# Clamps of a weight preparation on GpSimd and a new, strictly followed order for the attention of an attention, soft MoE and MLP kernel

## The chip, the cores and the metric

The kernel runs on one core of a Trainium2 chip. The time is that of one execution on the device, in microseconds. A core has a matmul engine (TensorE, PE in the rows; its weight loads are PEld), three others that work in parallel with it (VectorE or DVE, ScalarE or ACT, GpSimd or POOL), and SyncE (SP), whose queue issues nearly all DMA transfers here. Each engine takes its instructions strictly in the order in which the program gives them, and waits on semaphores for the others.

## What is computed

```python
# 4 batches, 8 heads, 576 tokens, head size 64; float32 throughout
q_rot, k_rot = rotate(q), rotate(k)              # rotary embedding
scores = q_rot @ k_rot.T / 8
attn = exp(scores - scores.max(-1)); attn /= attn.sum(-1) + 1e-9
x = (attn @ v) -> (2304, 512)                    # heads side by side
logits = x @ phi                                 # 32 slots, 8 experts x 4
d = softmax(logits, over tokens); slot_in = d.T @ x
slot_out[e] = relu(slot_in[e] @ w1[e]) @ w2[e]   # 512 -> 1024 -> 512
x = softmax(logits, over slots) @ slot_out
out = relu(x @ w_in) ** 2 @ w_out                # 512 -> 2048 -> 512
```

w_in and w_out come as 64-bit floats, and the kernel turns them into float32.

## The kernel before

The attention works on 16 pairs of heads. The two heads of a pair lie in the upper and lower 64 partitions, so that two matmuls with 64 rows of contraction run side by side. For each pair:

- rope_pair (L547) rotates k and q with six operations of 128x576 on GpSimd (for pair 0 on VectorE). parts_pair (L571) splits each into a rounded part "hi" (ScalarE) and a rest "lo" (GpSimd), so that f32r products of parts make up a more exact product; windows (L629) keeps copies of the last 64 keys.
- max_unit (L642): a hi x hi product for each of four blocks of 128 keys and two halves of the queries, and one for the last 64 keys of both halves: nine products, each a pair of f32r matmuls (the last has two pairs) into one of three PSUM bank pairs, the "ring"; VectorE reduces each to a maximum (L665). max_rows (L670) transposes the maxima (L684), and SyncE writes them as a row "mrow" into the operand tile (L703).
- st_unit (L727): the score products of the same nine units. Each takes three pairs of f32r matmuls for the parts (L738) and one that subtracts the maximum (L745), twice as many for the last unit; ScalarE takes the exponential of the ring bank (L758) into one of a few probability buffers, whose key in the planner is pk. GpSimd adds the buffers of units 0 and 1 (L766).
- pv_unit (L774): the product with V in float32, two matmuls of 64 columns side by side (L789); the unit of the last 64 keys has its own form (L784). norm (L795): column sums (L813) and their inverse on VectorE. logits (L849): products with phi (L863, L868) and transposes of the result (L886). After each fourth pair slots_in (L902) updates the slots.

free (L1153) loads expert weights in pieces of 512 KB into buffers as these come free: ten of a ring, w0 to w9, others in tiles that the attention gives up at its end (arena, tO, tEa, tEb, tLa, tLb, pb). prepare (L1194) converts an eighth of the weights that stay in DRAM as float32: load, scale to z (ScalarE, L1213), low half (ScalarE, L1220), clamp of z (VectorE, L1225), upper half (ScalarE, L1232), shift and merge (VectorE, L1237), store (SyncE, L1244). Behind the attention experts (L1412) multiplies with w1 and w2, whose later pieces are loaded as buffers come free, and mlp (L1610) does the rest.

What sets the order: every operation goes into a Plan (L30) with its engine, a cost in us, a due time, and what it reads and writes. emit (L292) simulates the engines with these costs: of the operations that are ready and can start within 0.208 us (AHEAD, TensorE) of the earliest, it issues the one that is due first. For the attention the due times come from ORDER, a table of ranks by function and engine (retime, L221); they are preferences. "soft" operations give way when a hard one is due in the meantime. In gaps of TensorE that the plan foresees, emit puts filler products (L1880). What is issued is a fixed program; the chip knows nothing of ranks and costs.

Of the kernel before, what the change touches and what calls it, by code (L numbers as in the profile page):

```python
# [38 lines left out]
class Plan:  # L39
# [14 lines left out]
            0, 2, 3, 4  # L54
        ),
        ("first_loads", "ACT", None): (
            1,
        ),
        ("first_loads", "DVE", None): (
            20,  # L60
        ),
        ("rope_pair", "DVE", None): (
            11, 12, 15, 13, 16, 18
        ),
        ("warm_up", "PE", None): (
            14,
        ),
        ("parts_pair", "ACT", None): (
            17, 19, 55, 79, 117, 150, 194, 224, 273, 305, 346, 361, 429, 454, 526, 531, 631, 633, 721, 724, 815, 818, 910, 914, 1013, 1015, 1101, 1104, 1193,
            1196, 1261, 1268  # L70
        ),
        ("parts_pair", "POOL", None): (
            22, 28, 60, 86, 124, 160, 199, 230, 279, 314, 359, 369, 435, 460, 532, 543, 637, 648, 732, 742, 825, 836, 922, 929, 1023, 1032, 1112, 1120, 1202,
            1210, 1273, 1281
        ),
        ("rope_pair", "POOL", None): (
# [4 lines left out]
        ),  # L81
        ("load", "SP", None): (
            36, 99, 173, 176, 180, 237, 240, 242, 322, 323, 327, 373, 377, 379, 468, 471, 473, 557, 561, 565, 659, 662, 665, 753, 755, 758, 846, 849, 852, 942,
            946, 949, 1043, 1045, 1047, 1131, 1133, 1136
        ),
        ("windows", "ACT", None): (
            23, 30, 82, 81, 156, 132, 226, 217, 309, 296, 406, 408, 499, 502, 606, 608, 698, 701, 791, 794, 884, 887, 988, 990, 1078, 1081, 1168, 1171, 1265,
            1275, 1331, 1332
        ),
# [7 lines left out]
        ),  # L97
        ("max_unit", "DVE", None): (
# [6 lines left out]
        ),  # L105
        ("max_rows", "DVE", None): (
            43, 47, 48, 56, 58, 59, 122, 129, 133, 205, 215, 218, 297, 306, 308, 395, 409, 412, 487, 500, 503, 593, 609, 610, 688, 702, 703, 779, 795, 796, 874,
            888, 889, 975, 991, 993, 1068, 1082, 1083, 1156, 1172, 1173, 1249, 1264, 1266, 1348, 1352, 1353, 1403, 1409, 1414
        ),
        ("max_rows", "PE", "f"): (  # L110
            46, 57, 127, 211, 302, 405, 498, 605, 697, 790, 883, 987, 1077, 1167, 1260, 1349, 1406
        ),
        ("max_rows", "SP", None): (
            51, 62, 134, 136, 219, 222, 312, 317, 415, 417, 509, 510, 615, 618, 707, 710, 800, 803, 893, 896, 997, 1000, 1087, 1090, 1177, 1180, 1270, 1274, 1358,
            1355, 1422, 1418
        ),
        ("max_rows", "ACT", None): (
            52, 63
        ),
        ("<lambda>", "SP", None): (  # L120
            65,
# [91 lines left out]
            0: 1514, 1: 1524, 2: 1526  # L213
        },
        (None, "ACT", None): {
            0: 1525
        },
    }
    kind = None
# [26 lines left out]
    def op(self, engines, fn, due, reads=(), writes=(), kb=None, after=None, spare=None, take=None, give=None, wait=0.0, behind=None, tok=None, mode=None, like=None, soft=False):  # L246
# [7 lines left out]
        i = len(self.ops)  # L254
# [1717 lines left out]
```

## Time and profile before

| | us |
|---|---|
| median of 3 runs | 565.54 |
| lowest, highest | 565.38, 566.69 |
| the profiled execution | 565.09 |
| its span, first to last instruction | 563.3 |
| TensorE busy in it | 544.0 |
| VectorE, ScalarE, GpSimd busy | 398.6, 295.7, 229.9 |

The span covers first to last instruction; the 1.8 us of the execution beside it are its start and end. A view "windows" gives the busy time of each engine in a stretch, "timeline" the instructions in order of time. In a timeline row the first number is the start, the second the time taken, "xN" the count of like instructions merged into the row, and the brackets hold the idle time of the engine ahead of it and what ended it. A float32 matmul of the program appears as two in the trace, one of f32r as one. Ends of matmuls are modelled; starts are measured.

### The profile page before, as it was taken

The numbers are of one execution on the slowest core, as the hardware profiler recorded it, in microseconds if no ns is written. First come the engines' busy times: TensorE is split into PE (matmuls) and PEld (weight loads), VectorE is DVE, ScalarE is ACT, GpSimd is POOL, SyncE is SP. The second block draws the span as 40 slices with busy tenths as digits, with TensorE's granted clock in tenths as the row PEclk, the third lists the DMA queues.
The fourth block names the chain that finished last, engine by engine and source line by source line (L and its number), as shares of the span: only waits on it lengthen the run. The fifth ranks groups of instructions, "written<-read, shape, count | busy, mean of one in ns | idle before, by whom it ended". The sixth has DMA issues, their size and how long they took to land.

```text
span 563.3 us, 13271 instructions
## 1 busy us (share of the span) xinstructions
PE 544.0 (97%) x5406; PEld 416.7 (74%) x5406; DVE 398.6 (71%) x878; ACT 295.7 (52%) x568; POOL 229.9 (41%) x178
## 2 busy tenths in 40 slices
PE   4999999999999999999999999999999999999996
PEld 3656666566665666666642258999999999999996
DVE  6587788888897887876468748965775595554553
ACT  2334545664555655544426548975944564354440
POOL 4999999988889788723610000000000000000000
PEclk9999999999999999999999999999999999999999
DMA  7447796877784357222989997132200220000333
GB/s 237 139 132 184 167 249 188 221 192 195 210 219 117 93 144 201 100 99 101 338 295 396 409 401 255 39 111 76 76 1 1 76 76 2 1 1 1 113 113 112
DMA packets 37741, 85.68 MB, mean 152 GB/s; under 512 B 12176, under 2 KB 12848, under 8 KB 36528
## 3 DMA queue, kind: packets, MB, share of 16 engines
q1 hardware_dynamic: 37398, 84.24, 48.3%
q8 instruction: 42, 0.69, 0.5%
q10 hardware_dynamic: 282, 0.59, 0.4%
q14 instruction: 19, 0.16, 0.1%
HBM read 77.92 MB, written 6.82 MB: 150 GB/s over the span
## 4 chain that ended last, share of the span: by engine, by line
PE 81%; DMA 9%; DVE 5%; POOL 2%; ACT 1%; issue 1%; SPq 0%; DVEq 0%
PE bank L1806 35%; PE bank L738 11%; PE obank L789 11%; PE bank L654 5%; PE bank L813 5%; PE bank L745 3%; PE obank L1736 3%; DVE mcol L665 2%; DMA w__1345<-in_w_dram 2%; DMA tEb<-in_w_dram 2%; DMA tLb<-in_w_in_dram 2%; PE obank L784 2%; PE bank L886 2%; DMA ident<-in_ident_dram 1%; POOL arena L543 1%; DMA w__448<-in_w_dram 1%
## 5 line engine op out<-in xcount | busy, mean ns | idle before, releaser
L758 ACT ACTIVATE tO<-bank 128x576 f32<-128x576 f32 x140 | 84.2, 650 | 84.4 <-PE bank L745 83.3
L665 DVE TENSOR_REDUCE mcol<-bank 128x2 f32<-128x576 f32 x144 | 103.2, 749 | 22.6 <-PE bank L654 13.1
L543 POOL TENSOR_TENSOR arena<-arena 128x576 f32<-128x576 f32 x78 | 111.0, 1444 | 8.8 <-DMA arena<-in_qk_dram 8.0
L1806 PE MATMUL bank<-w,tEb 128*128 128x256 f32 x864 | 106.5, 279 | 0.1
L1806 PEld LDWEIGHTS bank<-w,tEb 128*128 128x128 f32 x864 | 103.5, 188 | 2.4 <-issue 1.6
L789 PE MATMUL obank<-tO,pb 128*64 128x288 f32 x496 | 74.8, 419 | 0.0
L766 POOL TENSOR_TENSOR pb<-tO 128x576 f32<-128x576 f32 x30 | 42.9, 1430 | 31.0 <-ACT tO L758 29.4
L1806 PE MATMUL bank<-w,tEa 128*128 128x256 f32 x432 | 53.0, 278 | 0.0
L1806 PEld LDWEIGHTS bank<-w,tEa 128*128 128x128 f32 x432 | 51.6, 188 | 1.2 <-issue 1.2
L1806 PE MATMUL bank<-w,tO 128*128 128x256 f32 x432 | 51.6, 277 | 0.0
L1806 PEld LDWEIGHTS bank<-w,tO 128*128 128x128 f32 x432 | 51.1, 188 | 0.0
L789 PEld LDWEIGHTS obank<-tO,pb 128*64 128x64 f32 x496 | 29.8, 136 | 22.7 <-issue 9.3
L1747 ACT ACTIVATE pb<-obank 128x384 f32<-128x384 f32 x47 | 21.7, 495 | 36.8 <-PE obank L1736 36.8
L1747 ACT ACTIVATE w__1091<-obank 128x384 f32<-128x384 f32 x48 | 21.8, 491 | 36.5 <-PE obank L1736 36.2
L654 PEld LDWEIGHTS bank<-tEb 64*128 64x128 f32 x180 | 16.3, 184 | 21.5 <-DVE mcol L665 4.4
L813 PE MATMUL bank<-tO,ones 128*32 128x288 f32 x224 | 31.9, 409 | 0.0
L654 PE MATMUL bank<-tEb 64*128 64x288 f32 x180 | 30.5, 355 | 0.7 <-DVE mcol L665 0.5
L819 DVE STREAM_TRANSPOSE bank<-bank 128x288 f32<-128x288 f32 x32 | 15.9, 496 | 19.2 <-PE bank L813 15.8
L543 POOL TENSOR_TENSOR tLb<-arena,tEb 128x576 fp32r<-128x576 f32 x20 | 28.6, 1448 | 1.3 <-ACT tEb L577 1.3
L738 PE MATMUL bank<-tEb 64*128 64x288 f32 x180 | 28.5, 313 | 0.3 <-DVE mcol L665 0.2
L1736 PE MATMUL obank<-x,tO 128*128 128x384 f32 x95 | 26.8, 336 | 0.5 <-DVE tO L1664 0.5
L738 PE MATMUL bank<-tLb,tEb 64*128 64x288 f32 x180 | 26.6, 292 | 0.0
(299 smaller groups left out, 1095.2 us busy)
## 6 DMA issues: line engine op xcount, KB each, us to landing
arena<-in_qk_dram SPq DMA_DIRECT2D x14, 576.0 KB
arena<-in_qk_dram SPq DMA_DIRECT2D x12, 512.0 KB
arena<-in_w_dram SPq DMA_DIRECT2D x8, 512.0 KB
pb<-in_v_dram SPq DMA_DIRECT2D x12, 320.0 KB
arena<-in_qk_dram SPq DMA_DIRECT2D x3, 1152.0 KB
tLb<-in_w_in_dram SPq DMA_DIRECT2D x3, 1024.0 KB
pb<-in_w_in_dram SPq DMA_DIRECT2D x3, 1024.0 KB
w__448<-in_w_dram SPq DMA_DIRECT2D x4, 512.0 KB
```

What stands on the lines that cost most here:

```text
L543: ENG[e].tensor_tensor(out=o, in0=x, in1=y, op=how)
L654: nc.tensor.matmul(on_ring(tok)[:, j, 0:HQ], lhsT=x[rows], rhs=hi[rows, 0, HALF[c]], start=(u < BOTH or c == 0), stop=(u < BOTH or c == 1),)
L665: lambda e: nc.vector.tensor_reduce(out=mcol[:, h, :, u], in_=on_ring(tok)[:, :, 0:HQ], op=ALU.max, axis=AX.X),
L738: nc.tensor.matmul(st[:, j, 0:HQ], lhsT=w[rows], rhs=q[y][rows, HALF[c]], start=(i == 0 and (u < BOTH or c == 0)), stop=False,)
L745: nc.tensor.matmul(st[:, j, 0:HQ], lhsT=pick[rows, w : w + 128], rhs=mrow[rows, HALF[c]], start=False, stop=(u < BOTH or c == 1),)
L758: lambda e: nc.scalar.activation(out=pr, in_=on_ring(tok)[:, :, 0:HQ], func=AF.Exp, scale=0.125),
L766: lambda e: nc.gpsimd.tensor_tensor(out=acc, in0=one, in1=pr, op=ALU.add),
L789: nc.tensor.matmul(BANKS[6 + h][o, 0:HQ], lhsT=vr[:, u, j, :], rhs=pr[:, j, :], start=(h == 0 and u == 0), stop=(h == 1 and u == 3))
L813: nc.tensor.matmul(sm[QUAD[2 * j + w], 0:HQ], lhsT=one, rhs=x[:, j, :], start=(i == 0), stop=(i + w + 2 > last))
L1736: lambda e, i=i, t0=t0: nc.tensor.matmul(BANKS[i][:, 0:384], lhsT=wst_of()[:, 128 * fc : 128 * fc + 128], rhs=cst_of()[:, t0 : t0 + 384], ...
L1747: lambda e, i=i, h=h: nc.scalar.activation(out=rg_of()[:, 0, h], in_=BANKS[i][:, 0:384], func=AF.Relu),
L1806: nc.tensor.matmul(BANKS[c][:, cols], lhsT=gt[:, x, 128 * c : 128 * c + 128], rhs=wo[:, fc % 2, y, cols], start=(fc % FQ == 0 and i == 0 a ...
```

## The change

Five edits. ORDER has new ranks, and they are now followed strictly: retime collects (rank, operation), and emit takes the next of this list, asserts that it is ready, and issues it, with no choice; the greedy rule is left for what has no rank, that is all behind the attention. The clamp of prepare goes from VectorE to GpSimd, and is no longer soft. Each st_unit names its probability buffer pk among its writes, where it did so for the last two pairs alone. Three VectorE costs of the plan are raised. The plan holds GpSimd while VectorE runs an operation with "lock". Behind the planner's part the diff shows in turn rope_pair (the shift of prepare gets the same lock), max_rows, st_unit, two places of norm, and prepare.

```diff
     ORDER = {
         ("first_loads", "SP", None): (
-            0, 2, 3, 4
+            1, 4, 20, 8
         ),
...
+        ("prepare", "POOL", None): (
+            605, 610, 692, 778, 940, 1010, 1051, 1193
+        ),
...
     def retime(self):
         count = {}
+        self.turn = []
...
             if kind or n in ranks:
-                self.ops[i] = (*o[:2], 0.1 * ranks[n], *o[3:])
+                self.turn.append((ranks[n], i))
...
+        turn = [i for _, i in sorted(self.turn, reverse=True)]
         while ready:
             cand = []
-            for i in ready:
+            ranked = turn.pop() if turn else None
+            assert ranked is None or ranked in ready, (ranked, self.kinds[ranked])
+            for i in ready if ranked is None else (ranked,):
...
-            if i in self.soft:
+            if i in self.soft and ranked is None:
...
+            alone = i in self.locks and e == "DVE"
+            if alone:
+                start = max(start, free.get("POOL", 0.0))
             end = start + self.ops[i][0][e]
+            if alone:
+                free["POOL"] = end
...
-                    spare={"DVE": T["sprope"]}, like=one,
+                    spare={"DVE": T["sprope"]}, like=one, lock=True,
...
-            {"DVE": 0.25},
+            {"DVE": 0.31},
...
-            [ck, pk] if p in LATE else [ck], take="ring", tok=tok, mode="r",
+            [ck, pk], take="ring", tok=tok, mode="r",
...
-        ring_op({"DVE": 1.1}, inverse, g, [("sm", n)], ["r9"], give="ring", tok=tok)
+        ring_op({"DVE": 1.16}, inverse, g, [("sm", n)], ["r9"], give="ring", tok=tok)
...
-            {"DVE": 0.8 if p < TURNED else 0.4},
+            {"DVE": 0.97 if p < TURNED else 0.4},
...
         op(
-            {"DVE": 0.4},
-            lambda e: nc.vector.tensor_scalar(
+            {"POOL": 0.6},
+            lambda e: nc.gpsimd.tensor_scalar(
                 out=z_of(), in0=z_of(), scalar1=F64_HUGE, scalar2=-F64_HUGE, op0=ALU.min, op1=ALU.max
             ),
-            g + 6.1, (), [zk], soft=True,
+            g + 6.1, (), [zk],
         )
```

Line numbers of the changed kernel are 14 higher from max_unit on (a score product is at L752 and L759, a maximum product at L668, V at L803 and L798). In the middle of the attention TensorE's order before, in pair 8, has the products with V (L789) of three key blocks in one group, between maximum products of the next pair (L654):

```order
L654 MATMUL bank_93<-tEb 128x288 x2
L654 MATMUL bank_91<-tEa 128x288 x2
L789 MATMUL obank_94<-tO_84,pb 64x288 x2
L789 MATMUL obank_94<-tO_83,pb 64x288 x4
L654 MATMUL bank_93<-tEa 128x288 x2
L654 MATMUL bank_93<-tEa,wins 128x288 x2
```

Now, behind the maxima of pair 10, blocks stand alone or in twos between f32r products:

```order
L668 MATMUL bank_92<-tEa 128x288 x2
L798 MATMUL obank_94<-tO_84,pb 64x288 x2
L798 MATMUL obank_95<-tO_84,pb 64x288 x2
L803 MATMUL obank_95<-tO_83,pb 64x288 x2
L668 MATMUL bank_93<-tEa 128x288 x2
L752 MATMUL bank_91<-tEb 128x288 x2
L752 MATMUL bank_91<-tLb,tEb 128x288 x2
L752 MATMUL bank_91<-tEb,tLb 128x288 x2
L759 MATMUL bank_91<-tEa,pick 128x288 x2
L668 MATMUL bank_92<-tEa 128x288 x2
L803 MATMUL obank_95<-tO_83,pb 64x288 x2
```

What moved: the same matmuls change kind more often. At the start, TensorE's order before has the first maximum product of pair 1 (L654 on tEb) behind the last score product of pair 0:

```order
L738 MATMUL bank_93<-tEa,tLa 128x288 x2
L738 MATMUL bank_93<-tEa,wins 128x288 x2
L745 MATMUL bank_93<-tEb,pick 128x288 x4
L654 MATMUL bank_91<-tEb 128x288 x2
L654 MATMUL bank_92<-tEb 128x288 x2
L789 MATMUL obank_94<-tO_83,pb 64x288 x2
```

Now it stands behind the third:

```order
L752 MATMUL bank_91<-tEa 128x288 x2
L752 MATMUL bank_91<-tLa,tEa 128x288 x2
L752 MATMUL bank_91<-tEa,tLa 128x288 x2
L759 MATMUL bank_91<-tEb,pick 128x288 x2
L668 MATMUL bank_92<-tEb 128x288 x2
L752 MATMUL bank_93<-tEa 128x288 x2
```

The maximum products of pair 1 moved ahead by some six score units. On SyncE, at the end of the attention, before has the last mrow write (tEa<-mrow, pair 15) and behind it 16 pieces of expert weights, these and four more to pb:

```order
L703 DMA tEa<-mrow_125 1x5x128 x2
L1174 DMA arena<-in_w_dram 128x1024 x4
L1174 DMA tLb_3540<-in_w_dram 128x1024
L1174 DMA tEb_3551<-in_w_dram 128x1024
L1174 DMA tLb_3540<-in_w_dram 128x1024
L1174 DMA tEb_3551<-in_w_dram 128x1024
L1174 DMA tEa_3657<-in_w_dram 128x1024 x2
L1174 DMA tO_3715<-in_w_dram 128x1024 x2
```

Now 19 pieces stand behind it; the first of them:

```order
L717 DMA tEa<-mrow_125 1x5x128 x2
L1188 DMA arena<-in_w_dram 128x1024
L1188 DMA tO_3629<-in_w_dram 128x1024
L1188 DMA tLb_3631<-in_w_dram 128x1024
L1188 DMA tO_3629<-in_w_dram 128x1024
L1188 DMA tEb_3702<-in_w_dram 128x1024
L1188 DMA arena<-in_w_dram 128x1024 x2
```

Pieces for the ring buffers and for tO that were loaded earlier moved to the end, and three more now lie behind the last mrow write.

## Rows read from the trace of the kernel before

**Rows 1.** The page: span, TensorE's share, the chain by engine.
```profile
span 563.3 us, 13271 instructions
PE 544.0 (97%) x5406; PEld 416.7 (74%) x5406; DVE 398.6 (71%) x878; ACT 295.7 (52%) x568; POOL 229.9 (41%) x178
...
PE 81%; DMA 9%; DVE 5%; POOL 2%; ACT 1%; issue 1%; SPq 0%; DVEq 0%
```

**Rows 2.** Windows: stretch, length, engines (busy, count), clock, DMA share, GB/s.
```profile
60.00:80.00 20.00, 20.00 (x232) 12.60 (x230) 15.04 (x39) 8.88 (x17) 19.92 (x16) 1.00 0.84 208
...
200.00:220.00 20.00, 20.00 (x258) 13.63 (x258) 15.63 (x41) 12.87 (x26) 16.32 (x12) 1.00 0.65 160
```

**Rows 3.** Timeline of TensorE, 122 to 128 us: start, time, instruction.
```profile
122.33 0.29 PE L745 MATMUL bank<-tEa,pick 64*128 64x288 f32 x2
122.55 1.68 PE L789 MATMUL obank<-tO,pb 128*64 128x288 f32 x12
124.16 0.40 PE L654 MATMUL bank<-tEb 64*128 64x288 f32 x2
...
125.91 0.29 PE L745 MATMUL bank<-tEb,pick 64*128 64x288 f32 x2
126.04 0.29 PE L654 MATMUL bank<-tEb 64*128 64x288 f32 x2
126.27 0.71 PE L789 MATMUL obank<-tO,pb 128*64 128x288 f32 x4
126.91 0.40 PE L654 MATMUL bank<-tEb 64*128 64x288 f32 x2
127.14 0.29 PE L738 MATMUL bank<-tEa 64*128 64x288 f32 x2
```

**Rows 4.** Timeline, 119 to 130 us: around two groups of column sums.
```profile
119.73 0.60 PE L886 MATMUL bank<-ident,pb 128*128 128x128 f32 x4
...
121.70 0.40 PE L654 MATMUL bank<-tEb 64*128 64x288 f32 x2
...
128.53 0.43 PE L813 MATMUL bank<-pb,ones 128*32 128x288 f32 x1
...
129.64 0.53 PE L654 MATMUL bank<-tEb 64*128 64x288 f32 x4
```

**Rows 5.** Line L684, 130 to 170 us: minimum, median, maximum in ns; first, last start.
```profile
L684 PE MATMUL bank<-ident,m x3: 274/275/275, 135.6 to 168.0; 128*10 128x128 f32 x3
```

**Rows 6.** Timeline of VectorE and TensorE at the start, pairs 1 and 2.
```profile
26.59 6.08 DVE L665 TENSOR_REDUCE mcol<-bank 128x2 f32<-128x576 f32 x9 [5.47 <-PE bank L654]
...
43.28 0.40 PE L654 MATMUL bank<-tEb 64*128 64x288 f32 x2
43.95 0.40 PE L654 MATMUL bank<-tEb 64*128 64x288 f32 x2 [0.27 <-DVE mcol L665]
```

**Rows 7.** Groups by line, VectorE: count, busy us, mean ns, idle before.
```profile
L1225 DVE TENSOR_SCALAR w__1091<-w__1091 128x512 f32<-128x512 f32 x8 | 7.8, 974 | 0.0
```

**Rows 8.** Groups by line, GpSimd.
```profile
L543 POOL TENSOR_TENSOR arena<-arena 128x576 f32<-128x576 f32 x78 | 111.0, 1444 | 8.8 <-DMA arena<-in_qk_dram 8.0
...
L1481 POOL MEMSET si<- 128x512 f32 x1 | 0.5, 525 | 11.4 <-PE bank L1470 11.4
```

**Rows 9.** Timeline of the SyncE queue at the attention's end.
```profile
268.45 1.42 SPq L703 DMA_DIRECT2D tEa<-mrow  x2
...
295.77 0.33 SPq L1174 DMA_DIRECT2D w__448<-in_w_dram  x1
```

**Rows 10.** Windows of 5 us there, columns as in rows 2.
```profile
285.00:290.00 5.00, 4.38 (x43) 2.44 (x40) 3.63 (x14) 1.55 (x5) 0.00 (x0) 1.00 0.56 174
...
300.00:305.00 5.00, 5.00 (x52) 1.43 (x44) 4.22 (x18) 3.66 (x12) 0.00 (x0) 1.00 1.03 402
```

More of the change, by code (lines that the diff above doesn't have):

```diff
@@ L53 @@
         ("first_loads", "SP", None): (
-            0, 2, 3, 4
+            1, 4, 20, 8
         ),
         ("first_loads", "ACT", None): (
-            1,
+            0,
         ),
         ("first_loads", "DVE", None): (
-            20,
+            17,
         ),
         ("rope_pair", "DVE", None): (
-            11, 12, 15, 13, 16, 18
+            2, 3, 13, 5, 6, 10
         ),
         ("warm_up", "PE", None): (
-            14,
+            7,
         ),
         ("parts_pair", "ACT", None): (
-            17, 19, 55, 79, 117, 150, 194, 224, 273, 305, 346, 361, 429, 454, 526, 531, 631, 633, 721, 724, 815, 818, 910, 914, 1013, 1015, 1101, 1104, 1193,
@@ L70 @@
-            1196, 1261, 1268
+            14, 11, 53, 62, 139, 132, 213, 198, 287, 298, 379, 375, 437, 447, 536, 538, 626, 601, 709, 716, 801, 802, 904, 909, 989, 1002, 1097, 1076, 1187, 1177,
+            1268, 1277
         ),
         ("parts_pair", "POOL", None): (
-            22, 28, 60, 86, 124, 160, 199, 230, 279, 314, 359, 369, 435, 460, 532, 543, 637, 648, 732, 742, 825, 836, 922, 929, 1023, 1032, 1112, 1120, 1202,
-            1210, 1273, 1281
+            15, 12, 76, 74, 175, 177, 217, 199, 288, 310, 399, 390, 450, 460, 554, 548, 627, 609, 710, 717, 808, 809, 926, 947, 1012, 1013, 1115, 1101, 1346,
@@ L85 @@
+            948, 997, 1126, 1037, 1119, 1201, 1128, 1189
         ),
         ("windows", "ACT", None): (
-            23, 30, 82, 81, 156, 132, 226, 217, 309, 296, 406, 408, 499, 502, 606, 608, 698, 701, 791, 794, 884, 887, 988, 990, 1078, 1081, 1168, 1171, 1265,
-            1275, 1331, 1332
+            18, 42, 70, 116, 140, 251, 223, 349, 332, 430, 397, 535, 480, 550, 584, 726, 725, 705, 759, 917, 921, 845, 968, 1071, 1066, 1124, 1151, 1250, 1304,
+            1377, 1324, 1348
         ),
         ("max_unit", "PE", "r"): (
[6 rows of a table removed]
[5 rows of a table added]
@@ L115 @@
-            1355, 1422, 1418
+            51, 77, 142, 141, 233, 242, 302, 299, 394, 405, 511, 512, 590, 589, 697, 684, 785, 784, 882, 875, 966, 965, 1089, 1065, 1149, 1154, 1264, 1265, 1341,
+            1336, 1415, 1416
         ),
         ("max_rows", "ACT", None): (
-            52, 63
+            45, 58
         ),
         ("<lambda>", "SP", None): (
-            65,
+            193,
         ),
         ("natural_table", "SP", None): (
-            71, 74, 78
+            102, 101, 219
@@ L125 @@
         ),
         ("load_v", "SP", None): (
-            5, 6, 7, 8, 9, 10, 80, 83, 89, 91, 95, 101, 146, 148, 152, 155, 166, 170, 249, 252, 255, 266, 270, 275, 363, 453, 552, 655, 747, 841, 935, 1036, 1125,
-            1214, 1302, 1368
+            80, 9, 81, 19, 67, 50, 73, 99, 159, 100, 109, 162, 253, 197, 212, 234, 227, 241, 296, 268, 308, 315, 368, 353, 436, 510, 542, 677, 813, 912, 961,
+            1036, 1135, 1203, 1331, 1385
         ),
         ("st_unit", "PE", "r"): (
[6 rows of a table removed]
[6 rows of a table added]
         ),
@@ L174 @@
+            1384, 1499, 1484, 1458, 1504, 1475, 1457, 1528, 1526, 1503, 1511, 1527, 1525, 1523, 1524
         ),
         ("logits", "PE", "q"): (
-            220, 318, 411, 504, 611, 704, 797, 890, 994, 1084, 1174, 1267, 1360, 1417, 1478, 1502
+            194, 295, 400, 477, 591, 707, 753, 865, 979, 1045, 1155, 1247, 1334, 1419, 1480, 1491
         ),
         ("logits", "DVE", None): (
-            225, 320, 416, 505, 616, 708, 801, 894, 998, 1088, 1178, 1272, 1364, 1423, 1483, 1506
+            195, 301, 401, 482, 592, 719, 756, 866, 983, 1046, 1160, 1249, 1343, 1424, 1492, 1493
@@ L187 @@
+            1487, 1488, 1514, 1515
         ),
         ("prepare", "SP", None): (
-            390, 517, 483, 604, 589, 669, 684, 789, 775, 855, 870, 986, 971, 1050, 1064, 1166
+            407, 749, 503, 915, 674, 895, 704, 998, 835, 1016, 937, 1118, 953, 1322, 1092, 1382
         ),
         ("prepare", "ACT", None): (
-            431, 436, 463, 549, 556, 570, 619, 624, 653, 728, 745, 757, 808, 822, 839, 932, 938, 953, 1002, 1006, 1034, 1108, 1123, 1135
+            546, 499, 608, 537, 579, 653, 679, 771, 782, 763, 918, 941, 876, 923, 967, 970, 1019, 1029, 1044, 1043, 1088, 1174, 1200, 1255
+        ),
@@ L199 @@
         ),
         ("slots_in", "ACT", None): (
-            520, 528, 535, 902, 905, 913, 918, 1282, 1280, 1285, 1287, 1511, 1515, 1513, 1518
+            484, 485, 869, 872, 879, 891, 1074, 1371, 1337, 1338, 1372, 1498, 1506, 1517, 1518
         ),
         ("slots_in", "PE", "f"): (
-            548, 550, 931, 933, 1404, 1405, 1516, 1519
+            490, 492, 899, 900, 1403, 1404, 1505, 1507
         ),
         ("slots_in", "PE", "q"): (
-            566, 569, 948, 952, 1424, 1426, 1522, 1527
+            529, 539, 927, 928, 1439, 1440, 1516, 1521
@@ L208 @@
         ),
         (None, "PE", None): {
-            0: 1512, 1: 1521
+            0: 1501, 1: 1512
         },
         (None, "DVE", None): {
-            0: 1514, 1: 1524, 2: 1526
+            0: 1502, 1: 1513, 2: 1520
         },
         (None, "ACT", None): {
-            0: 1525
+            0: 1519
         },
@@ L244, in __init__, with op @@
         self.soft = set()
-    def op(self, engines, fn, due, reads=(), writes=(), kb=None, after=None, spare=None, take=None, give=None, wait=0.0, behind=None, tok=None, mode=None, like=None, soft=False):
+        self.locks = set()
+        self.turn = []
+    def op(self, engines, fn, due, reads=(), writes=(), kb=None, after=None, spare=None, take=None, give=None, wait=0.0, behind=None, tok=None, mode=None, like=None, soft=False, lock=False):
         i = len(self.ops)
@@ L256, in op @@
             self.soft.add(i)
+        if lock:
+            self.locks.add(i)
         deps = set()
@@ L1240, in prepare @@
             ),
-            g + 6.3, [zk, kl, ks], [dk], soft=True,
+            g + 6.3, [zk, kl, ks], [dk], soft=True, lock=True,
         )
```

33 lines of the change are left out of this document (15 added, 18 removed), and 74 rows, old and new, of the table ORDER.

## The prediction

> **What bounds the kernel now.** I read the page first [rows 1]: TensorE is busy 97% of a span of 563.3 us, and the chain that ended last runs on it for 81%. A busy share says little here, since the ends of matmuls are modelled, so the next view is the windows [rows 2]. From 60 us on TensorE shows 20.00 of 20 us busy while VectorE has 15 to 16 and GpSimd falls from 19.9 to 16.3 of 20: neither of the two is the bound of the middle of the attention. Whether TensorE works or waits there is seen in the starts of its matmuls [rows 3]. Three spacings occur. Pairs of the f32r products (maxima at line 654, scores at 738 and 745, two matmuls of 64 rows side by side) start 0.13 us apart (125.91 to 126.04). The f32 products with V (line 789) take 0.64 us for one key block (x4, 126.27 to 126.91) and 1.61 us for three (x12, 122.55 to 124.16), so 0.485 us for each further block and 0.155 us for the group as such. The third spacing is the change of kind: the last f32r pair before a V group takes 0.23 us instead of 0.13 (126.04 to 126.27), and the first one after it 0.23 us too (126.91 to 127.14). A pass from f32r to V and back thus costs 0.10 + 0.155 + 0.10 = 0.355 us, in which nothing is computed.
>
> That this is all there is can be summed for one head pair of the middle. 50 f32r pairs x 0.13 = 6.5; eight V blocks x 0.485 = 3.9; the block that serves both halves about 0.6; transposes, logits and the first column sums 1.97 (119.73 to 121.70) and the second column sums 1.11 (128.53 to 129.64) [rows 4]; the transpose of the row maxima 0.1; five f32r groups x 0.20 and five V groups x 0.155 = 1.8. Sum 16.0 us. The transpose of the maxima (line 684) recurs twice from 135.6 to 168.0 us, 16.2 us each [rows 5]. So 0.2 us of a pair is waiting. In the middle **TensorE is the bound, and only less work or fewer changes of kind can shorten it.**
>
> Behind the attention the transfers of expert weights are the chain: after the last maxima went out at 268.45 us the issues follow as buffers come free, the first refill of the ring of weight buffers is issued at 295.77 us, and from 300 us the DMA runs at 402 GB/s with share 1.03 [rows 9, 10]. All that follows is in the same order on every engine before and after, so an end of the attention that moves by x moves the end of the kernel by about x.
>
> **The change part by part.**
>
> *Order on TensorE.* The counts of matmuls with work in them are the same. But counted down to the last attention product, the order of before has 76 groups of f32r products and 66 of V blocks; after has 107 and 83. Before repeats one pattern (three V blocks together, then singles); after has 48 groups of a single V block where before has 32. Groups of column sums and logits go from 31 to 33, transposes from 21 to 24. The price: 31 x 0.20 = 6.2, 17 x 0.155 = 2.6, five others at about 0.1 = 0.5: **+9.3 us**, nearly all of it in pairs 4 to 13, where the sum above leaves 0.2 us of waiting in a pair to hide it in. The lower bound is the part that is inside the groups alone, 2.6 us (if the 0.20 us at the f32r sides were waits that come once however often kinds change); the upper one, all of a 0.355 us pass for each of the 31, is 11.0. I take 9.3, since both sides of [rows 3] show the same 0.23 at a group of one block and of three.
>
> The Trainium skill (TensorEngine Tiling (Array Packing), Tiling Modes, Key Properties) says that a change of tiling mode drains TensorE, and it speaks against this change. Its page TensorE: Matmul & The Clock Gate (Part 2, step DRAIN) gives about 128 cycles for a drain; as an estimate from these pages two drains a pass at 2.4 GHz (granted clock 1.00 in [rows 2]) are 0.11 us, 3.3 us for 31 passes instead of 9.3. The trace has 0.355 us a pass, so the sum goes by the trace.
>
> *Order at the start.* VectorE has nothing to do for 5.47 us before the first maxima of pair 1 at 26.59 us [rows 6]. Before issues all score products of pair 0 first; after puts the first maximum product of pair 1 behind three of them and moves the last rotation of pair 1 on GpSimd ahead of a subtraction. The first reduction can then start some 3 us earlier. What this removes on TensorE are waits like that from 43.28 to 43.95 us, 0.67 instead of 0.13 [rows 6]; with the shorter ones of this sort up to 60 us they make some 3 us, and starting pair 1 sooner can save 2 more. Bounds 0 to -5; I take **-3**.
>
> *Order of the loads.* Between the last two mrow writes (of pairs 14 and 15) after has seven pieces of 512 KB where before has four, and behind the last one 19 instead of 16. Three more pieces are 1.57 MB, 3.9 us at 402 GB/s. The DMA has a hole at 285 to 290 us, where its share is 0.56 (2.2 us idle) [rows 10]. So 0 to 1.7 us arrive late at the ring; I take **+0.8**. In the middle a run of six w1 pieces now stands ahead of one mrow write on SP; behind that wait the score products of one pair, and it is the third rival's place.
>
> *Clamps.* Eight TENSOR_SCALARs leave VectorE, where they took 7.8 us, 0.974 each [rows 7]. GpSimd has no such row; the nearest are a MEMSET of the same 128x512, 0.525 us, and a TENSOR_TENSOR of 128x576, 1.444 us, that is 1.28 us for 512 columns [rows 8]. Eight are 4 to 10 us of GpSimd, about 8 with 1.0 each, halfway since it reads one operand. They stand between pairs 6 and 13, some 115 us in which GpSimd has 16.3 of 20 us filled [rows 2], so 20 us are free. Behind a clamp on GpSimd wait the next rotation and column sum, one or two operations ahead of need; VectorE's 7.8 us back bring nothing where TensorE doesn't wait for it. Cost 0; if the cover is gone, 8 us over eight pairs, at most 1 a pair. A gain on the path could be 1 at most.
>
> *Score products wait for their buffer.* The key pk is added to the planner's writes. The matmuls write a PSUM bank and not that buffer, so no wait of the chip comes from it; it only limits which tables can be issued. The changed prices (0.31, 1.16, 0.97) and the lock are the planner's too and decide only filler products while the table lasts. 0.
>
> *Sum.* The profiled execution took 565.09 us (its span 563.3 and 1.8 around it). 565.1 + 9.3 - 3 + 0.8 = 572.2. The median of the three runs is 565.54, 0.45 above it: **572.6 us.**
>
> **The rivals.**
>
> *Faster: changes of kind cost little.* If the 0.20 us beside a group were waits that a strict order meets in any case, only 17 x 0.155 = 2.6 us are added, and with the whole 5 us of the start won the time is 563.1 us. For it speaks that VectorE and GpSimd are above 75% busy, so a smoother mix could hide such waits; against it that 16.0 of 16.2 us are accounted for without them. It decides from an f32r price below 0.05 us a group. The drain alone that the Trainium skill's two pages give would lead close to this: by that estimate 563.8.
>
> *No change.* The start gives back 5, the transfers nothing, and the passes that fall beside waits of the first and the last pairs (four of the sixteen) are free, a quarter of 9.3: 565.5 + 7 - 5 = 567.5, and with 2 more from the last pair 565.5. This needs everything to go well at once.
>
> *Much slower: the strict table starves TensorE.* An order without choice lets one late transfer stop the queue. The place is pair 8: six pieces ahead of its mrow write are 3.1 MB, 7.8 us at 402 GB/s, against some 4 us of products between the issue and the first score product; 4 us of waiting there, and once more where V blocks of pair 0 are loaded behind the mrow writes: 576 to 581. It decides when pieces are issued later than some 8 us ahead of the write.
>
> **How the numbers follow.** About 0.3% (1.7 us) is what a measurement of this kernel can tell from no change. The forecast (568 to 576) has 0.60, starvation 0.15, no change 0.10, faster 0.15. Slower is 0.75 in sum. The likeliest time is 572.5 us. The range from 564 to 579 leaves out the faster case and the end of starvation, some 0.18; its width comes from 2.6 to 11.0 of the changes of kind, 0 to -5 of the start and up to 4 of a late write.
>
> **What would show it.** The changed profile should have the transpose of the maxima some 16.8 us apart in pairs 4 to 13 instead of 16.2; the same 0.13, 0.23, 0.64 spacings; VectorE's first reduction of pair 1 near 23.5 us; the refill of the ring issued near 302 us instead of 295.77, and the MLP unchanged behind it. I am wrong if a change of kind takes less than 0.1 us in the new order, if the transposes stay 16.2 us apart, or if TensorE waits over 1 us for an mrow write or V in the middle.

## The result, and the profile after

The changed kernel takes 569.07 us (median of 8 executions, 568.48 to 570.60), the kernel before 566.48 in the same comparison (8, 565.38 to 567.83): a ratio of 1.0054, 95% interval 1.0038 to 1.0070, so 3 us slower. (A ratio leaves out executions that are more than 1.5% above the fastest of their kernel.) The forecast was 572.5 within 564 to 579, "slower" with 0.75. The direction holds, and the loss is less than half of the 7 us that were worked out.

The profiled execution took 569.22 us, 4.1 more than that of before, which with 565.09 lies below all eight of its executions here. About 1 us of the 4.1 is scatter between executions. The page of the changed kernel, against [rows 1]:

```profile
span 567.4 us, 13320 instructions
PE 549.6 (97%) x5416; PEld 416.3 (73%) x5416; DVE 396.1 (70%) x870; ACT 297.1 (52%) x568; POOL 234.2 (41%) x186
...
PE 89%; DMA 6%; DVE 2%; ACT 1%; issue 0%; DVEq 0%; ACTq 0%; SPq 0%
```

The chain that ended last runs on TensorE for 89% of the span instead of 81%, and VectorE's part fell from 5% to 2%, that of transfers from 9% to 6%. So TensorE does more in a row and waits less: both are in the result. The windows, against [rows 2, 10]:

```profile
60.00:80.00 20.00, 19.97 (x238) 13.62 (x238) 16.27 (x39) 10.44 (x20) 19.41 (x15) 1.00 0.63 133
200.00:220.00 20.00, 20.00 (x232) 12.78 (x234) 16.82 (x37) 11.93 (x25) 18.20 (x15) 1.00 0.75 186
285.00:290.00 5.00, 5.00 (x65) 2.67 (x57) 3.75 (x16) 1.40 (x3) 1.20 (x1) 1.00 0.96 346
300.00:305.00 5.00, 5.00 (x52) 1.56 (x48) 4.22 (x15) 3.37 (x10) 0.00 (x0) 1.00 1.01 383
```

The hole of the DMA at 285 to 290 us is filled (share 0.96, was 0.56). The price of a change of kind is what it was; TensorE around a single V block (start, time, instruction), against [rows 3]:

```profile
125.08 0.30 PE L668 MATMUL bank<-tEb,wins 64*128 64x288 f32 x2
125.31 0.71 PE L803 MATMUL obank<-tO,pb 128*64 128x288 f32 x4
125.94 0.40 PE L752 MATMUL bank<-tEa 64*128 64x288 f32 x2
126.18 0.29 PE L752 MATMUL bank<-tLa,tEa 64*128 64x288 f32 x2
```

0.23 into the V block, 0.63 in it, 0.24 behind it. The transposes of the maxima, against [rows 5]:

```profile
134.47 0.28 PE L698 MATMUL bank<-ident,m 128*10 128x128 f32 x1
...
150.52 0.27 PE L698 MATMUL bank<-ident,m 128*10 128x128 f32 x1
...
168.11 0.27 PE L698 MATMUL bank<-ident,m 128*10 128x128 f32 x1
```

They recur after 16.1 and 17.6 us, 16.8 on average, as foretold for these two. But over pairs 4 to 13 the distance went from 16.8 (which the two intervals of [rows 5] had not shown) to 17.2 only. VectorE's first reduction of pair 1, SyncE's last mrow write and the first refill of the ring, against [rows 6, 9], and the clamps (count, busy us, mean ns, idle before), against [rows 7]:

```profile
24.42 0.76 DVE L679 TENSOR_REDUCE mcol<-bank 128x2 f32<-128x576 f32 x1 [2.49 <-ACT tO L772]
```

```profile
270.46 1.41 SPq L717 DMA_DIRECT2D tEa<-mrow  x2
...
299.03 0.33 SPq L1188 DMA_DIRECT2D w__812<-in_w_dram  x1
```

```profile
L1239 POOL TENSOR_SCALAR w__1293<-w__1293 128x512 f32<-128x512 f32 x8 | 5.3, 667 | 0.0
```

**Where the time went.** I took the starts of all matmuls of the attention and summed TensorE's time by group. A group of n pairs of f32r products without a wait takes 0.131 (n - 1) + 0.33 us, entry and exit included; what it takes beyond that is counted as waiting (early pairs at half pace too). Stretches go from the transpose of the maxima of one pair to that of another; before, then after:

| stretch | length, us | f32r groups | time in them | of it waits | V groups | time in them |
|---|---|---|---|---|---|---|
| start to pair 1 | 33.8, 32.8 | 7, 7 | 16.1, 14.0 | 6.9, 4.8 | 4, 4 | 2.5, 2.5 |
| pair 1 to 3 | 31.7, 31.4 | 7, 12 | 16.0, 15.2 | 3.1, 0.7 | 8, 9 | 9.0, 9.2 |
| pair 3 to 6 | 53.8, 53.3 | 16, 23 | 25.8, 25.4 | 1.7, 0.2 | 12, 18 | 13.5, 14.4 |
| pair 6 to 10 | 66.4, 67.7 | 20, 30 | 30.8, 32.2 | 0.6, 0.3 | 16, 20 | 17.9, 17.6 |
| pair 10 to 15 | 80.3, 84.1 | 24, 32 | 38.5, 39.4 | 1.2, 0.4 | 21, 28 | 22.6, 24.6 |
| pair 15 to the end | 23.4, 23.5 | 2, 3 | 6.9, 6.4 | 0.8, 0.1 | 5, 4 | 6.6, 6.5 |
| sum | 289.4, 292.8 | 76, 107 | 134.1, 132.6 | 14.3, 6.5 | 66, 83 | 72.1, 74.8 |

The V groups take 2.7 us more, which is 17 x 0.155. The f32r groups should take 31 x 0.20 = 6.2 us more and take 1.5 less, because 7.8 us of waits inside them are gone. With 1.9 us more of filler products at the start and 0.4 of column sums the attention ends 3.4 us later. The first expert product starts 3.3 us later and the first of the MLP 4.1, so some 0.9 is lost behind the attention.

A part of the 6.9 and 4.8 us of the first row isn't waiting for another engine. The f32r pairs of the first score products start 0.24 us apart until 23.95 us in before and until 22.61 in after. By these spacings half pace makes 1.7 of the 6.9 us and 1.2 of the 4.8. The granted clock from 20 to 25 us, in after and in clamp_moved (TensorE's order of before; the trace of before itself has no record of the clock ahead of 24.1 us) is a mean of its two levels, 0.50 and 1.00:

```profile
20.00:25.00 5.00, 4.75 (x40) 3.82 (x40) 1.91 (x5) 3.04 (x6) 4.45 (x4) 0.71 0.30 68
```

```profile
20.00:25.00 5.00, 5.00 (x37) 4.14 (x37) 0.55 (x2) 2.84 (x5) 4.46 (x4) 0.55 0.25 40
```

### The profile page after: what moved, and what is told of

The parts are those of the page before. It is cut to its first block, busy times and chain, and to the rows that moved or that the text cites. A ratio compares the mean times of both kernels' runs of the same rounds, so it can differ in the third digit from the quotient of the medians.

```text
span 567.4 us, 13320 instructions
## 1 busy us (share of the span) xinstructions
PE 549.6 (97%) x5416; PEld 416.3 (73%) x5416; DVE 396.1 (70%) x870; ACT 297.1 (52%) x568; POOL 234.2 (41%) x186
## 4 chain that ended last, share of the span: by engine, by line
PE 89%; DMA 6%; DVE 2%; ACT 1%; issue 0%; DVEq 0%; ACTq 0%; SPq 0%
PE bank L1820 35%; PE bank L752 13%; PE obank L803 13%; PE bank L668 6%; PE bank L827 6%; PE bank L759 4%; PE obank L1750 3%; DMA w__1403<-in_w_dram 2%; PE obank L798 2%; DMA tEb<-in_w_dram 2%; DMA tLb<-in_w_in_dram 2%; PE bank L900 2%; PE bank L1521 2%; DMA arena<-in_qk_dram 1%; PE bank L983 1%; PE bank L877 1%
## 5 line engine op out<-in xcount | busy, mean ns | idle before, releaser
L772 ACT ACTIVATE tO<-bank 128x576 f32<-128x576 f32 x140 | 87.5, 650 | 104.0 <-PE bank L759 84.1
L679 DVE TENSOR_REDUCE mcol<-bank 128x2 f32<-128x576 f32 x144 | 104.5, 753 | 32.5 <-PE bank L668 25.2
L803 PE MATMUL obank<-tO,pb 128*64 128x288 f32 x496 | 78.6, 423 | 0.0
L780 POOL TENSOR_TENSOR pb<-tO 128x576 f32<-128x576 f32 x30 | 43.0, 1434 | 25.8 <-ACT tO L772 25.8
L803 PEld LDWEIGHTS obank<-tO,pb 128*64 128x64 f32 x496 | 28.4, 135 | 23.2 <-issue 12.1
L827 PE MATMUL bank<-tO,ones 128*32 128x288 f32 x224 | 32.2, 410 | 0.0
L752 PE MATMUL bank<-tEb 64*128 64x288 f32 x180 | 30.2, 332 | 0.0
L668 PE MATMUL bank<-tEb 64*128 64x288 f32 x180 | 29.0, 340 | 0.1
L668 PEld LDWEIGHTS bank<-tEb 64*128 64x128 f32 x180 | 16.1, 184 | 17.0 <-DVE mcol L679 5.7
L752 PEld LDWEIGHTS bank<-tEb 64*128 64x128 f32 x180 | 16.9, 184 | 14.0 <-DVE mcol L679 4.8
## 6 DMA issues: line engine op xcount, KB each, us to landing
arena<-in_qk_dram SPq DMA_DIRECT2D x14, 576.0 KB
```

The lines of the kernel that those rows point to most:

```text
L668: nc.tensor.matmul(on_ring(tok)[:, j, 0:HQ], lhsT=x[rows], rhs=hi[rows, 0, HALF[c]], start=(u < BOTH or c == 0), stop=(u < BOTH or c == 1),)
L679: lambda e: nc.vector.tensor_reduce(out=mcol[:, h, :, u], in_=on_ring(tok)[:, :, 0:HQ], op=ALU.max, axis=AX.X),
L752: nc.tensor.matmul(st[:, j, 0:HQ], lhsT=w[rows], rhs=q[y][rows, HALF[c]], start=(i == 0 and (u < BOTH or c == 0)), stop=False,)
L772: lambda e: nc.scalar.activation(out=pr, in_=on_ring(tok)[:, :, 0:HQ], func=AF.Exp, scale=0.125),
L780: lambda e: nc.gpsimd.tensor_tensor(out=acc, in0=one, in1=pr, op=ALU.add),
L803: nc.tensor.matmul(BANKS[6 + h][o, 0:HQ], lhsT=vr[:, u, j, :], rhs=pr[:, j, :], start=(h == 0 and u == 0), stop=(h == 1 and u == 3))
```

## Experiments

A kernel of the experiments issues a list of all operations of the plan, with the fillers ahead of each; the list of before and that of after, issued in this way, give the instructions of these two kernels on every engine. So the raised prices, the lock and the pk key do nothing by themselves: what differs on the chip is the list and the engine of the clamps.

```diff
-        turn = [i for _, i in sorted(self.turn, reverse=True)]
+        turn = [x if isinstance(x, tuple) else (x, 0, -1) for x in reversed(self.REPLAY)]
...
-            ranked = turn.pop() if turn else None
+            ranked, fillers, slot = turn.pop()
```

Ratios are to before in the same comparison (medians 565.7 to 566.2). The expectations count the starts of transposes from a zero 0.2 us later than the views.

### The clamps alone, in both orders

Before's list with the clamp of after, and after's with the clamp of before:

```diff
-            {"DVE": 0.4},
-            lambda e: nc.vector.tensor_scalar(
+            {"POOL": 0.6},
+            lambda e: nc.gpsimd.tensor_scalar(
```

> The order of before, unchanged on every engine, with the eight clamps alone moved from VectorE to the same places of GpSimd's order. My theory: the clamps are worth nothing either way, since TensorE waits neither for GpSimd nor for VectorE's 7.8 us there: 566.5 us, within 0.5 of before. The rival (the clamps are what changed the time, by filling GpSimd in front of a rotation) gives after's time, 568 to 569; one in which VectorE's freed 7.8 us shorten the pairs gives 564 to 565.5.

Measured: 566.3 us, 1.0011 (0.9996 to 1.0027): nothing.

> The order of after with the eight clamps back on VectorE, at the same places of the order of issue. My theory: 569.1 us, as after. If the clamps on GpSimd cost after 2.6 us, this gives 566.5; if the smaller waits of after (10.2 us instead of 20.6, by my pricing of its groups) come from a VectorE that is relieved of them, it gives 571 to 577.

Measured: 572.86 us, 1.0119 (1.0086 to 1.0151), 4 us slower than after. My theory was wrong here. All of it is lost at one place; VectorE, then TensorE:

```profile
122.13 0.76 DVE L679 TENSOR_REDUCE mcol<-bank 128x2 f32<-128x576 f32 x1 [0.61 <-PE bank L668]
122.81 2.36 DVE L1239 TENSOR_SCALAR w__1293<-w__1293 128x512 f32<-128x512 f32 x2
125.09 1.41 DVE L679 TENSOR_REDUCE mcol<-bank 128x2 f32<-128x576 f32 x2
```

```profile
125.89 0.40 PE L752 MATMUL bank<-tEa 64*128 64x288 f32 x2 [1.69 <-DVE mcol L679]
```

After's list has two clamps in a row between two reductions; on VectorE they hold the reductions up for 2.36 us, the ring isn't emptied, and TensorE waits 1.69 us. And it pays again afterwards (windows, the granted clock in the third column from the end):

```profile
124.00:126.00 2.00, 0.31 (x6) 0.11 (x4) 2.00 (x3) 0.98 (x2) 0.88 (x1) 1.00 1.00 208
126.00:128.00 2.00, 2.00 (x20) 1.29 (x22) 1.97 (x4) 1.22 (x2) 0.00 (x0) 0.96 1.05 250
128.00:130.00 2.00, 2.00 (x21) 1.16 (x22) 0.79 (x2) 0.65 (x1) 1.79 (x2) 0.50 0.88 324
130.00:132.00 2.00, 2.00 (x24) 1.08 (x18) 0.69 (x3) 0.00 (x0) 2.00 (x2) 0.69 0.58 138
```

TensorE was busy for 0.31 of 2 us, and from 128 us its granted clock is 0.50 (1.2 instead of 2.4 GHz) until within the next window. From pair 6 to 10 this kernel takes 71.3 us, after 67.7.

### The price of a change of kind, added to before and to after

In before's list the last V block of 17 groups moves behind the first f32r product that follows, as here:

```diff
-L803 MATMUL obank_94<-tO_83,pb 64x288 x6
+L803 MATMUL obank_94<-tO_83,pb 64x288 x4
 L668 MATMUL bank_91<-tEb 128x288 x2
 L668 MATMUL bank_91<-tEb,wins 128x288 x2
+L803 MATMUL obank_94<-tO_83,pb 64x288 x2
```

> The order of before, clamps on VectorE; in pairs 4 to 13 the last V block of 17 groups is moved behind the first f32r product that follows, so that the groups of V blocks go from 66 to 83 and those of f32r products from 76 to 93. Nothing else moves. My theory (a pass costs 0.355 us and is added to the time, since TensorE is the bound): 17 x 0.355 = 6.0, so 572.5 us. The rival (a change of kind falls into waits that are there in any case, 8.2 us of them between 60 and 265 us): 0 to 2 us more, 566.5 to 568.5.

Measured: 569.38 us, 1.0065 (1.0050 to 1.0080), 3.5 us slower. In its trace the attention ends 4.0 us later: the 6.0 of the price, less 2.1 us of waits inside f32r groups (14.3 to 12.2). So the price is real, and a third of it falls where TensorE would have waited. Neither theory had that.

The same edit on 17 groups of after:

> The order of after, in which the last V block of 17 more groups, from pair 3 to the last, is moved behind the first f32r product that follows: groups of V blocks from 83 to 100, of f32r products from 107 to 124. In the order of before the same edit cost 4.0 us of the 6.0 that 17 passes of 0.355 us come to, and the waits inside f32r groups fell by 1.8 us (14.3 to 12.5, all groups summed). My theory: a pass costs its full price, less the waits that it happens to fill; after has only 0.9 us of such waits left behind pair 3, so 5 to 6 us are added: 574 to 575. The rival (a finer order saves about a third of its price wherever it stands): 573 us.

Measured: 576.39 us, 1.0194 (1.0173 to 1.0215), 7 to 8 us slower than after. The waits rise from 6.5 to 7.5 instead of falling. Where no waits are left to be filled, a pass costs its full price and a little more.

### Taking changes of kind out of after

22 groups of V blocks of after wait for the next one:

```diff
 L668 MATMUL bank_93<-tEb 128x288 x2
-L803 MATMUL obank_94<-tO_84,pb 64x288 x2
 L668 MATMUL bank_91<-tEb 128x288 x2
 L752 MATMUL bank_92<-tEb 128x288 x2
 L752 MATMUL bank_92<-tLb,tEb 128x288 x2
 L752 MATMUL bank_92<-tEb,tLb 128x288 x2
 L759 MATMUL bank_92<-tEa,pick 128x288 x2
 L668 MATMUL bank_93<-tEb 128x288 x2
-L803 MATMUL obank_94<-tO_84,pb 64x288 x2
+L803 MATMUL obank_94<-tO_84,pb 64x288 x4
```

> The order of after; 22 groups of V blocks are held back until the next group of V blocks, behind at most three f32r products, so that the groups of V blocks go from 83 to 61 and those of f32r products from 107 to 91. Nothing else moves. My theory (the price of a pass is paid in full, and the small waits that after has lost stay lost): 22 x 0.155 + 16 x 0.20 = 6.6 us less than after, 562.5 us, faster than before too. The rival (the finer mix is itself what took the waits away, so that longer groups bring them back): 567 to 569 us.

Measured: 577.23 us, 1.0213 (1.0158 to 1.0268), 8 to 9 us slower than after instead of 6.6 faster: the clearest miss. Its four executions lie from 574.7 to 582.3 us, and the profiled one is the slowest of them; in it the waits inside f32r groups are 21.2 us, in after 6.5. A place with four V blocks in a row, first TensorE, then VectorE and ScalarE, then the windows:

```profile
90.28 0.40 PE L668 MATMUL bank<-tEb 64*128 64x288 f32 x2 [0.47 <-ACT tO L772]
90.61 3.85 PE L803 MATMUL obank<-tO,pb 128*64 128x288 f32 x16
```

```profile
94.84 0.76 DVE L679 TENSOR_REDUCE mcol<-bank 128x2 f32<-128x576 f32 x1 [2.96 <-PE bank L668]
```

```profile
95.36 0.65 ACT L772 ACTIVATE tO<-bank 128x576 f32<-128x576 f32 x1 [4.99 <-PE bank L759]
```

```profile
88.00:90.00 2.00, 1.45 (x12) 0.99 (x12) 1.75 (x9) 0.90 (x2) 2.00 (x3) 1.00 0.74 200
...
92.00:94.00 2.00, 2.00 (x12) 0.88 (x8) 0.00 (x0) 0.00 (x0) 0.58 (x1) 0.50 1.13 259
```

Ahead of the long V group the f32r products run into the ring (0.47 us for an exponential, 1.45 of 2 us busy); then VectorE and ScalarE have nothing for 2.96 and 4.99 us, and the V group itself takes 3.78 us instead of 0.64 + 3 x 0.485 = 2.1, since the granted clock falls to 0.50 behind the short waits (in before and after it stays at 1.00 there). So here fewer changes of kind were not cheaper, because both other engines were no longer fed.

### Where in the program the loss lies

After's list up to the transpose of the maxima of pair 6 (cut), then what is left in before's order, and the reverse. How the first list is put together:

```python
REPLAY = AFTER[:cut] + [i for i in BEFORE if i not in AFTER[:cut]]
```

> The order of after up to the transpose of the maxima of pair 6, and behind it the order of before for all that is left; clamps on VectorE. In the traces after reaches this transpose 1.7 us earlier than before (117.5 against 119.2 us). My theory: the waits that after removes in front of it are gone for good, and the rest runs as in before: 1.7 us less than before, 564.3 us, faster than both kernels. The rival (the gain is an advance that the rest gives back, since transfers or GpSimd set its pace): 566, as before.

Measured: 580.79 us, 1.0277 (1.0258 to 1.0296). The hybrid has a fault of its own at the seam: eight expert pieces and three loads of q and k, which before issues earlier and after later, now come all at once. SyncE's queue, then GpSimd:

```profile
110.42 0.42 SPq L1188 DMA_DIRECT2D w__1403<-in_w_dram  x1
...
113.34 1.38 SPq L1188 DMA_DIRECT2D w__1483<-in_w_dram  x2
...
120.81 1.86 SPq L549 DMA_DIRECT2D arena<-in_qk_dram  x3
```

```profile
135.52 1.40 POOL L557 TENSOR_TENSOR arena<-arena 128x576 f32<-128x576 f32 x1 [14.39 <-DMA arena<-in_qk_dram]
```

From 110.42 us on eight pieces go out in a row, the q and k behind them at 120.81; GpSimd waits 14.39 us for these, and the next transpose comes 33 us after the last. So this run says nothing on the start of after; it does say what the third rival of the prediction, starvation by the order of the loads, costs when it strikes. So does the next one, in which only SyncE's pieces have before's places in after's list, two behind an mrow write for example:

```diff
 L717 DMA tEa<-mrow_125 1x5x128 x2
+L1188 DMA w__444<-in_w_dram 128x1024 x2
 L610 DMA pb<-in_v_dram 64x3x64
```

> The order of after, with the expert pieces of SyncE's queue placed among the mrow writes as in before: 16 instead of 19 behind the last of them. My theory: what after loses between the attention and the MLP (3.3 us behind at the first expert product, 4.2 at the first product of the MLP) comes back: 569.1 - 0.9 = 568.2 us. The rival (the ring of buffers sets when pieces are issued, and not their place in the queue): 569.1.

Measured: 578.57 us, 1.0242 (1.0207 to 1.0277). V comes too late (engine, line waited for: us, times, longest):

```profile
PE obank L803 <- DMA pb<-in_v_dram: 9.0, 3, 4.1
```

The places of the pieces belong to the rest of the list; the 0.9 us behind the attention can't be told from this run and stay as the comparison of the two traces has them.

> The other way round: the order of before up to the transpose of the maxima of pair 6, and behind it the order of after; clamps on GpSimd. From that transpose to the one of the last pair after takes 151.8 us, before 146.7, and 0.9 us more are lost behind the attention. My theory: the loss lies in this part alone, so before's 566 + 5.1 + 0.9 = 572 us, slower than after. The rival (after is slower here because it came early, and waits for what is not yet there): 569 at most.

Measured: 569.92 us, 1.0079 (1.0063 to 1.0095), between theory and rival. From pair 6 to 15 it takes 152.0 us, as after does (151.8; before 146.7): the loss lies in this part whatever stands ahead of it. What the start of after brings is the difference of the two ratios, 0.0025 or 1.4 us, with intervals that overlap, so a gain from it isn't shown.

### What took the waits away

Three V blocks move like this one:

```diff
-L803 MATMUL obank_94<-tO_83,pb 64x288 x4
...
+L803 MATMUL obank_94<-tO_83,pb 64x288 x2
 L668 MATMUL bank_92<-tEb 128x288 x2
...
 L668 MATMUL bank_93<-tEb 128x288 x2
+L803 MATMUL obank_94<-tO_83,pb 64x288 x2
 L668 MATMUL bank_92<-tEb 128x288 x2
```

> The order of before, in which three V blocks of pairs 1 and 2 (between 33.8 and 65.4 us) are moved from a group of two or three into the next place where one maximum product follows another: three passes more, 3 x 0.355 = 1.1 us by their price. That stretch has 3.1 us of waits inside f32r groups in before and 0.7 in after, where V blocks stand between the maximum products. My theory (a V block between two maximum products covers VectorE's reduction, which the ring otherwise waits for): the waits fall by about as much as the passes cost, 566 us, and the trace shows 1 us less of them. The rival (the waits don't depend on the places of V blocks): 567, with 3.1 us of waits left.

Measured: 566.99 us, 1.0003 (0.9983 to 1.0023). By time nothing is decided; in the trace this stretch is 0.9 us longer (32.6 against 31.7) and has 2.8 us of waits instead of 3.1. So three V blocks between maximum products pay 1.1 and bring 0.3: my theory isn't borne out, and which of after's moves takes away 2.4 us there stays open.

### A clamp that takes 6.7 us

Two tries at a better start. The first joins the lists as above, but with its cut at the transpose of pair 1:

> The order of after up to the transpose of the maxima of pair 1 only (32.8 us, before 33.8), where few loads lag behind the order of before (none of the expert pieces), then the order of before; clamps on VectorE. My theory: the 1.0 us won at the start stay won, and there is no hole of loads as in the hybrid that changed over at pair 6: 564.8 us. The rival (at such a seam what the start won is lost again at once, since pair 2 isn't ready): 565.8, as before.

The second adds fillers to before's list, on TensorE:

```diff
+L1894 MATMUL obank_94<-es 128x128
 L668 MATMUL bank_91<-tEa 128x288 x2
+L1894 MATMUL obank_94<-es 128x128
 L668 MATMUL bank_92<-tEa 128x288 x2
```

> The order of before with seven filler products more, between the maximum products of pair 0, where TensorE waits for VectorE's reductions 0.65 us apart. In the trace of before the f32r pairs of the first score products stand 0.24 us apart from 20.43 to 23.95 us, twice the 0.13 of later ones. If a busier TensorE ahead of them keeps the pace, 15 pairs take 2.0 us instead of 3.5, and pair 0 is 1.5 us earlier: 564.3 us. The rival (ScalarE's exponentials, 0.65 us each, set the pace of these units, or the fillers delay the maxima): 566 to 567.

The 12 executions of the first lie from 564.4 to 576.1 us, eleven of them above 572; those of the second from 563.8 to 576.0. Their ratios (1.0080, 1.0035 to 1.0124, and 1.0045, 1.0007 to 1.0083) leave out the slowest of these, and with them much of the effect, so they say little. The profiled executions took 573.38 and 575.20 us; none of the quick ones was profiled. In both profiles one thing stands out. VectorE, GpSimd and TensorE of the hybrid:

```profile
94.35 6.73 DVE L1239 TENSOR_SCALAR w__1096<-w__1096 128x512 f32<-128x512 f32 x1
101.00 0.48 DVE L833 STREAM_TRANSPOSE bank<-bank 128x288 f32<-128x288 f32 x1
```

```profile
95.33 7.01 POOL L557 TENSOR_TENSOR arena<-arena 128x576 f32<-128x576 f32 x5
```

```profile
102.17 0.61 PE L668 MATMUL bank<-tEb 64*128 64x288 f32 x2 [4.92 <-DVE mcol L679]
```

One clamp takes 6.73 us while GpSimd runs rotation after rotation, the reductions behind it wait, and TensorE waits 4.92 us. Behind that the granted clock is 0.50 in each window of 2 us from 102 to 108 us, though TensorE is busy (in before it is 1.00 there):

```profile
104.00:106.00 2.00, 2.00 (x20) 2.00 (x20) 1.94 (x5) 0.65 (x1) 0.00 (x0) 0.50 0.01 3
```

Six us at half pace are 3 us more, an estimate from these windows, so wait and clock together make some 8 us.

With the fillers the clamp takes 6.54 us and the wait 4.73. Their first score products do start 0.13 us apart, but only from 24.05 us on, when those of before had reached that pace too (23.95); and the fillers space the maximum products 1.26 us apart instead of 0.66. So that idea isn't borne out. The next lines show the same clamp and the same five rotations in before, then all eight clamps of before (minimum, median, maximum in ns):

```profile
94.04 1.11 DVE L1225 TENSOR_SCALAR w__1091<-w__1091 128x512 f32<-128x512 f32 x1
```

```profile
94.83 7.22 POOL L543 TENSOR_TENSOR arena<-arena 128x576 f32<-128x576 f32 x5
```

```profile
L1225 DVE TENSOR_SCALAR w__1091<-w__1091 x8: 409/1118/1464, 94.0 to 208.5; 128x512 f32<-128x512 f32 x8
```

Here it got through where one instruction of GpSimd ended and the next began. The Trainium skill (SBUF — State Buffer, SBUF: two separate sides) says that VectorE, in an operation of a 2-port mode or with two SBUF inputs, and GpSimd share a pair of ports under an exclusive lock: the one that starts first has it for its whole instruction, and the other is blocked fully. The trace agrees, with 6.73 us for a clamp that takes 0.41 at best, and goes further: in the hybrid the clamp, begun at 94.35 us, missed the ends of four instructions of GpSimd in a row (95.37 to 99.44 us) and ended just behind GpSimd's first pause, 0.08 us at 100.80; with the fillers it ended behind the like pause at 102.77. Four of the 79 executions of before in all comparisons took 572.0 to 572.8 us; none of them was profiled, so whether they met the same is not shown. The last run puts the theory to the test, with the clamp's edit from above in the first of the two kernels:

> The order of the hybrid that follows after up to pair 1's maxima (32.8 us) and before behind it, with the clamps on GpSimd instead of VectorE, nothing else changed. With the clamps on VectorE its profile shows one clamp (128x512, 409 ns at best in before) taking 6.73 us from 94.35 us, while GpSimd runs five rotations back to back (95.33 to 102.34 us), and 11 of its 12 executions take 572 to 576 us, one 564.4. My theory: the clamp is locked out while GpSimd works, and this is the whole of it: on GpSimd the clamps take 0.6 us each, TensorE no longer waits there, and the time is 564.5 to 566 us. The rival (VectorE waits there for something else, a transfer or ScalarE's copies, which the moved clamp leaves in place): 572 us and more.

Measured: 565.58 us (12 executions, 563.86 to 566.92), 0.9972 (0.9944 to 1.0000). The clamps, and the one in question on GpSimd:

```profile
L1239 POOL TENSOR_SCALAR w__1096<-w__1096 x8: 602/610/642, 94.6 to 210.8; 128x512 f32<-128x512 f32 x8
```

```profile
94.59 0.61 POOL L1239 TENSOR_SCALAR w__1096<-w__1096 128x512 f32<-128x512 f32 x1
95.16 7.03 POOL L557 TENSOR_TENSOR arena<-arena 128x576 f32<-128x576 f32 x5
```

Moving the clamps alone takes 8 us off this kernel and ends the scatter: the theory holds. It is also clearly faster than after. Against before a gain isn't shown: the interval ends at 1, the medians are 0.6 us apart, and two of before's executions at 572 us are in this comparison.

## Why the prediction was right, and where its size was wrong

- **Changes of kind, +9.3 us.** Right as a price: 0.23, 0.63 and 0.24 us stand in the new order, and the V groups take just 17 x 0.155 more. Adding 17 passes to after cost their full price. As a term of the sum it is complete only together with the next.
- **Waits taken away, -3 (0 to -5).** This is the step that was mis-sized. The waits inside f32r groups fell by 7.8 us (half pace included). 4.5 of them lie up to pair 3, where 1.9 us of fillers took back a part: 2.6 net, near the 3 foretold. The other 3.3 lie behind pair 3, and there the prediction hid nothing, since it saw "0.2 us of waiting in a pair"; even that would be 2 us over the ten pairs. The number came from two periods between 135.6 and 168.0 us; behind pair 3 before has 4.3 us of such waits, 1.7 of them from pair 3 to 6. The term is -5.9, not -3, and 9.3 - 5.9 gives the 3.4 us by which the attention ends later. That finer groups fill such waits is shown by the run that split groups of before (2.1 us); what took away those at the start stays open.
- **Loads, +0.8.** 0.9 in the traces, without an experiment that isolates it.
- **Clamps, 0, "a gain could be 1 at most".** Right for before's order by luck of the place (1.0011), wrong for after's, in which they would cost 4 us on VectorE. The row of [rows 7] gave a mean of 974 ns and hid 409 to 1464; that spread was the sign of two engines in each other's way, and the prediction priced the 7.8 us that VectorE gets back, not a clamp that holds VectorE up. Its "20 us are free" on GpSimd was read from one window of 20 us; the windows of before from 100 us to the last clamp at 208.5 leave some 14. As the clamps cost nothing there, the sum doesn't change.
- **Rivals.** "Changes of kind cost little" falls by the 7 to 8 us of 17 more passes in after; its other half, that a smoother mix hides waits, is true to a third in before (2.1 of 6.0 us). Starvation did not happen in after, but the two kernels with a foreign order of loads show it: TensorE waits 9.0 us for V in one, GpSimd 14.4 us for q and k in the other. "No change" missed by 3 us.
- **What would show it.** The refill of the ring came at 299.03, not 302; the first reduction of pair 1 at 24.42 (23.5 foretold). TensorE nowhere waits over 1 us for an mrow write or V.

## What to carry to other kernels

The price of a change of kind of matmul could be read from the spacing of starts, and it held in both orders; but in an order that feeds two other engines changes also buy something. Price both, and sum the waits over the whole program, not over the two cleanest periods. Where the same instruction has durations a factor of three apart, ask who shares something with it, and put small elementwise work on the engine that would otherwise lock it out. Joining two lists of issue fails where their loads are out of step: two such kernels lost 9 us and more against after, while the ones joined at pair 1 with the clamps moved, or the other way round at pair 6, lost nothing at the seam.

## What the hardware showed that was not expected

- An elementwise f32 operation of 128x512 from SBUF to SBUF (the clamp) takes 0.41 us on VectorE at best and 0.61 on GpSimd (602 to 642 ns in the last run; one of 1.05 us in after). Beside GpSimd instructions that follow each other without a pause it took 6.73 us on VectorE in one trace and 1.11 in another.
- Two waits cost TensorE more than their length: after one of 1.69 us (clamps back on VectorE) the granted clock stood at 0.50 in the window from 128 to 130 us and 0.69 in the next, and after one of 4.92 us (the hybrid) at 0.50 from 102 to 108 us, though TensorE was busy in these windows.
